# S4 convolution plus gated MLP on one core: early loads regrouped, GLU results accumulated into a copy of x, DMA transposes for half of the tokens, one more level of squares

## The chip, the cores and the metric

The kernel runs on one core of a Trainium2 chip. The core has five instruction streams: TensorE (PE, matrix products; its weight loads are listed apart as PEld), VectorE (DVE), ScalarE (ACT), GpSimd (POOL) and SyncE (SP, which here only issues DMAs). DMAs are issued from the queues of SP, ACT and POOL. The metric is the device time of one execution in microseconds (us), lower is better. The profile is of one execution, taken with the hardware profiler.

## The reference

The input `u` is a sequence of 2048 tokens with 512 channels in bfloat16. Cut to what matters:

```python
x = A_u                                   # (1, 2048, 512)
xn = _layernorm(x)
# branch A: a diagonal state space model with 128 modes per channel, as a long convolution
dt = exp(log_dt); P = exp(dt * (A_re + 1j*A_im) * l)      # l = 0..2047
K = einsum("dn,dnl,dn->dl", C, P, dt * B).real            # one kernel of 2048 taps per channel
yA = irfft(rfft(pad(xn)) * rfft(pad(K)))[:2048] + xn * Dskip
# branch B: a gated linear unit, 512 -> 1792 -> 512
yB = (sigmoid(xn @ w_gate) * (xn @ w_up)) @ w_down
return x + yA + yB
```

## The kernel before, in words

The program is a list of 1,266 tasks. Each is made with `_Plan.add`: an engine, a planned cost, a function that emits the instructions, and for some an alternative on another engine (`alt`). At the end they are emitted in the order that the tuple `TURN` lists, by task number; the tuple `OTHER` lists the tasks that take their alternative. Costs, ranks and `after` lists are for planning alone. Each engine executes its instructions in the emitted order, and the waits between engines come from the data: an instruction waits for what it reads, and for the buffer that it writes to be free. Buffers rotate: `zs` and `gs` share four buffers in SBUF, matmul results share four PSUM banks (`mbank`, pool `ps_m`), and the gate and up products have two pairs of banks of their own (`ps_gu`). A DMA from the SP or ACT queue takes one of eight semaphores in turn and waits until the DMA that had it eight issues before has landed; POOL's DMAs have eight of their own.

The stages, with the names and lines that matter below:

- **Loads** (`loads`, from line 356). `x` comes as `xg`, four groups of four token tiles of 128 rows. The S4 parameters come as `rawn` (A_re, A_im, B_re, B_im, C_re, C_im in slots 0 to 5), then the constants `ident`, `s1`, `s1e`, `s2`, `s2h`, `dsk`, and the GLU weights `W` (gate and up) and `wd` (down). POOL issues C, B, the constants and `dsk`.
- **Layer norm** (`layernorm`, from line 427). `stat` takes `bn_stats` of a tile on DVE (line 436). `rstd0` (lines 443 to 456) works out mean and inverse deviation for group 0 in small operations on DVE; `rstd` (lines 465 to 496) does the same for group 1 on POOL and for groups 2 and 3 together on DVE. `norm` (DVE, line 500) or `norm2` (ACT, line 505) normalises a tile in place. `turn` (line 510) transposes two tiles on PE into a PSUM bank `pt`, and an eviction writes them to `xnT`, the transposed input of the GLU, of which two buffers exist.
- **Parameters** (`params`). PE multiplies A and B by dt (`ptd`, `pb`) and transposes C (`ptp`); ACT and DVE make `exp` and `sin`/`cos` (`turns`, `frac`, `sincos`) of them, then the base rows of the tables in `B` and the multipliers in `M`.
- **Tables** (`tables`). For each of eight chunks of 64 channels the powers are built by doubling: `H` with 32 steps and `G` with 64 steps. A level is three DVE operations (`_level`, lines 1212 to 1214); `grow` replaces the even steps of the levels in `SQUARED` by squares, one ACT operation (line 859) and two on DVE (lines 861, 863). PE multiplies `G` by `H` into `pk` (line 947), which gives the convolution kernel, and on to its spectrum.
- **Spectrum of xn** (`spectrum_x1`, `spectrum_x2`). 32 products with `s1` give `pz`, evicted to `zs` and stored to `z_scr` in DRAM (SP); read back as `B<-z_scr` and multiplied again.
- **GLU** (`glu`, from line 741). Four groups, one after the other on PE: seven pairs of gate (`pg`) and up (`pu`) products of 128x512, sigmoid on ACT (line 778), product on DVE into `hT` (line 785), then `down` (line 756): for each tile 14 products of 128x512 into `po`, and one more with the identity that adds x itself, loaded again as `xt`. Of the 512 channels of `po`, the first 384 (`KEEP`) go through `gs` to the output (line 811, SP) and the last 128 stay on chip in `gl`.
- **Product and inverse** (`freq`, `outq`). The spectra are multiplied on DVE (line 1113), transformed back on PE (`pv`), and for the first 384 channels go through `v_scr` in DRAM and a product with `s2` (`py`, line 1172) to `M`, and from there by an accumulating DMA of POOL into the output (line 1192). The last 128 channels stay on chip: `vT` is transposed on PE into `ptv` (line 1157), copied, multiplied with `s2h` (line 1177), added to `gl` on DVE (line 1186), and `gl` is stored.

`evict` (lines 349 and 350) is the helper of nearly all copies out of PSUM: line 349 on ACT, line 350 on DVE. `dma` (line 342) is the helper of most DMAs.

## Time and profile before

| what | value |
|---|---|
| median of 3 runs | 268.0 us (266.95 to 268.19) |
| the profiled execution's own time | 269.39 us |
| its span, first to last event | 267.6 us |
| mean granted TensorE clock | 0.987 |
| DMA bytes | 43.05 MB, mean 161 GB/s |
| `out_dram<-gs`, SP | 32 issues of 48 KB, median 2.7 us to landing |
| `xt` loads, SP | 16 issues of 128 KB, median 3.3 us to landing |
| `out_dram<-M`, POOL | 24 issues of 64 KB, median 4.3 us to landing |

How to read it: a line of a group or a timeline gives the start and duration, or the busy time and mean of one, then the engine, the source line, the operation, and output<-input with shapes. "L350" is line 350 of the kernel before. The view by stage gives for each stretch the time in which each engine was busy, with the number of instructions in brackets. The chain of waits follows the work that ended last back to what released it.

### The profile page before, as it was taken

How to read it: one execution, taken by the hardware profiler on the slowest of the kernel's cores; microseconds unless marked ns; L12 is line 12 of the kernel's file. 1: busy time of each engine (PE TensorE's matmuls, PEld its weight loads, DVE VectorE, ACT ScalarE, POOL GpSimd, SP SyncE). 2: the span in 40 equal slices, each digit the busy share in tenths (PEclk: the TensorE clock that was granted, in tenths of full speed). 3: DMA queues.
4: the chain of work that ended last, by engine and by line, in shares of the span. 5: the costliest groups of instructions: out<-in, count | busy, mean ns of one | idle time of the engine just before them, and what ended most of it. 6: DMA issues, size and time to landing. Idle time of an engine off the chain costs nothing.

```text
span 267.6 us, 5570 instructions
## 1 busy us (share of the span) xinstructions
PE 236.7 (88%) x2039; PEld 136.9 (51%) x2064; DVE 246.8 (92%) x447; ACT 228.4 (85%) x362; POOL 48.1 (18%) x76
## 2 busy tenths in 40 slices
PE   0448999999999999899999999799999999969881
PEld 0325444444445544645545655565666576548660
DVE  2799999998999999999999999999999999998772
ACT  2669999999999886599999789899999889895860
POOL 9105982000000000000000000000000004436682
PEclk9999999999999999999999999999999999997997
DMA  6959981013801512225434489697989897997798
GB/s 162 249 142 315 316 253 50 0 40 88 345 20 40 179 48 63 76 94 150 148 98 118 110 227 229 160 270 188 252 215 281 201 219 167 223 242 138 98 133 88
DMA packets 68859, 43.05 MB, mean 161 GB/s; under 512 B 34704, under 2 KB 64416, under 8 KB 68320
## 3 DMA queue, kind: packets, MB, share of 16 engines
q1 hardware_dynamic: 63488, 39.99, 55.5%
q0 software_dynamic: 4896, 2.31, 8.0%
q10 hardware_dynamic: 448, 0.39, 0.7%
q8 instruction: 16, 0.26, 0.5%
q14 instruction: 11, 0.09, 0.1%
HBM read 24.33 MB, written 14.16 MB: 144 GB/s over the span
## 4 chain that ended last, share of the span: by engine, by line
PE 38%; DVE 25%; ACT 18%; DMA 10%; issue 5%; SPq 2%; ACTq 1%; DVEq 0%
PE pg L752 8%; PE pu L752 8%; PE po L756 7%; PE pk L947 4%; DMA B<-v_scr 4%; DMA zk_scr<-Z 3%; DVE tB L1212 2%; DVE stats L436 2%; DVE G L1213 2%; ACT M L349 2%; PE pv L1104 2%; ACT hT L778 2%; DMA rawn<-in_A_A_im_dram 2%; DVE G L1214 2%; DVE hT L785 2%
## 5 line engine op out<-in xcount | busy, mean ns | idle before, releaser
L752 PEld LDWEIGHTS <-W 128*128 128x128 bf16 x448 | 43.1, 98 | 50.9 <-issue 4.8
L1192 POOL DMA_DIRECT2D out_dram<-M x24 | 24.2, 1530 | 196.9 <-ACT M L349 191.2
L752 PE MATMUL pg<-xnT,W 128*128 128x512 bf16 x217 | 52.9, 384 | 1.0 <-ACT hT L778 0.3
L752 PE MATMUL pu<-xnT,W 128*128 128x512 bf16 x213 | 52.0, 379 | 0.9 <-DMA z_scr<-zs 0.2
L756 PE MATMUL po<-wd,hT 128*128 128x512 bf16 x217 | 51.6, 379 | 0.5
L756 PEld LDWEIGHTS <-hT 128*128 128x128 bf16 x224 | 21.6, 98 | 23.9 <-issue 0.4
L778 ACT ACTIVATE hT<-pg 128x1024 bf16<-128x1024 f32 x28 | 30.1, 1074 | 2.6 <-PE pg L752 1.2
L349 ACT ACTIVATE hT<-pu 128x1024 bf16<-128x1024 f32 x24 | 26.2, 1091 | 0.9 <-PE pu L752 0.8
L859 ACT ACTIVATE tB<-G 128x1024 bf16<-128x1024 bf16 (+1 forms) x17 | 24.5, 1442 | 2.7 <-DVE G L1214 1.5
L1214 DVE TENSOR_TENSOR G<-G,tB 128x1024 bf16<-128x1024 bf16 (+2 forms) x35 | 24.4, 702 | 0.4
L1213 DVE TENSOR_TENSOR G<-G,M 128x1024 bf16<-128x1024 bf16 (+1 forms) x42 | 22.0, 559 | 0.1
L947 PEld LDWEIGHTS <-G 128*128 128x128 bf16 x512 | 18.7, 100 | 5.9 <-DVE G L1214 2.7
L947 PE MATMUL pk<-H,G 128*128 128x64 bf16 x512 | 19.9, 196 | 1.9 <-DVE G L1214 0.9
L349 ACT ACTIVATE zs<-pz 128x512 bf16<-128x512 f32 x30 | 19.2, 670 | 2.4 <-PE pz L735 2.4
L1212 DVE TENSOR_TENSOR tB<-G,M 128x1024 bf16<-128x1024 bf16 (+2 forms) x27 | 21.0, 784 | 0.1
L1113 DVE TENSOR_TENSOR M<-XX,M 128x1024 bf16<-128x1024 bf16 x28 | 18.9, 686 | 0.3 <-ACT M L349 0.3
L1214 DVE TENSOR_TENSOR H<-H,tB 128x512 bf16<-128x512 bf16 (+2 forms) x24 | 18.6, 776 | 0.3
L349 ACT ACTIVATE M<-pkf 128x512 bf16<-128x512 f32 x28 | 17.9, 664 | 0.9 <-PE pkf L1093 0.9
L349 ACT ACTIVATE ksb<-pk 128x512 bf16<-128x512 f32 x28 | 17.3, 646 | 1.1 <-PE py L1172 0.5
L349 ACT ACTIVATE XX<-px 128x512 bf16<-128x512 f32 x26 | 16.0, 659 | 0.6 <-PE px L1046 0.5
L785 DVE TENSOR_TENSOR hT<-hT 128x1024 bf16<-128x1024 bf16 x24 | 16.3, 684 | 0.1
L1212 DVE TENSOR_TENSOR tB<-H,M 128x1024 bf16<-128x1024 bf16 (+1 forms) x16 | 15.2, 952 | 0.2
(211 smaller groups left out, 440.3 us busy)
## 6 DMA issues: line engine op xcount, KB each, us to landing
z_scr<-zs SPq DMA_DIRECT2D x32, 128.0 KB, 1.8
XX<-XX SPq DMA_DIRECT2D x28, 128.0 KB, 3.3
zk_scr<-Z SPq DMA_DIRECT2D x3, 1024.0 KB, 6.6
B<-zk_scr SPq DMA_DIRECT2D x12, 256.0 KB, 3.8
B<-v_scr SPq DMA_DIRECT2D x12, 256.0 KB, 4.0
xt<-in_A_u_dram SPq DMA_DIRECT2D x16, 128.0 KB, 3.3
B<-z_scr SPq DMA_DIRECT2D x8, 256.0 KB, 3.4
wd<-in_B_w_down_dram SPq DMA_DIRECT2D x1, 1792.0 KB, 14.4
```

The costliest lines, as they stand in the source:

```text
L349: return self.p.add("ACT", cost, lambda: nc.scalar.activation(out=dst(), in_=src(), func=ACT.Identity), alt=alt and ("DVE", alt[0], lambda ...
L752: nc.tensor.matmul(p[:, kk, :], w(kt, kk), xnT[:, kt, :], start=(kt == 0), stop=(kt == KT - 1))
L756: nc.tensor.matmul(po[:], hT[:, k, jj * 128:(jj + 1) * 128], wd[:, k, :], start=(k == 0), stop=False)
L778: e1 = add("ACT", 1.03, lambda hT=hT, k=k, pg=pg: nc.scalar.activation(out=hT[:, k:k + 2, :], in_=pg[:], func=ACT.Sigmoid), [m1] + held.ge ...
L785: prods.append(add("DVE", 0.69, lambda hT=hT, u=u, k=k: nc.vector.tensor_tensor(out=hT[:, k:k + 2, :], in0=hT[:, u:u + 2, :], in1=hT[:, k: ...
L859: a = add("ACT", 0.22 + 4 * h * k / 1200.0, lambda: nc.scalar.activation(out=sv(), in_=G[:, :, rs, src, :], func=ACT.Square, scale=float(2 ...
L947: nc.tensor.matmul(pk[:, r], G[:, comp, 8 * q + r].rearrange("p a h -> p (a h)"), H[:, comp, 8 * q + r].rearrange("p b h -> p (b h)"), sta ...
L1113: d = add("DVE", 0.69, lambda pp=pp, XX=XX, k1=k1, bs=bs: nc.vector.tensor_tensor(out=pp[:], in0=XX[:, :, bs, dx], in1=k1[:].to_broadcast( ...
L1192: self.p.add("POOL", 1.2, lambda j=j, o=o, ot=ot: nc.gpsimd.dma_start(out=o(), in_=ot[64 * j:64 * j + 64, :, :], accum_op=ALU.add), move=0 ...
L1212: lambda: [tt(out=tv()[:, c], in0=l[:, c], in1=mul[1][:, c], op=ALU.mult) for c in cs],
L1213: lambda: [tt(out=inner(o[:, c]), in0=inner(l[:, c]), in1=both(c), op=ALU.mult) for c in ones],
L1214: lambda: [tt(out=o[:, c], in0=o[:, c], in1=tv()[:, flip(c)], op=ALU.add) for c in cs],
```

## The change

- `loads`: POOL gets two tiny copies into a new tile `held`, which read the first group of x and the slots of A_re and A_im. In the new order they stand ahead of POOL's loads of C, B, `s1`, `s1e`, `s2` and `dsk`, which so are issued when x and A have landed.
- `layernorm`: tiles 1 and 3 may take their statistics on ACT (`stat_act`: a pass with a sum, a tiny scaling, a pass of squares with a sum), and do. The deviations of groups 2 and 3 move from DVE to POOL. The transposes of groups 2 and 3 are 32 transposing DMAs of 128x128 on SP, from `xg` straight to `xnT`; groups 0 and 1 keep PE and the eviction.
- `glu`: one DMA copies the first 384 channels of x from the input to the output in DRAM (`copied`, SP). The residual product with the identity covers the last 128 channels alone, and `xt` is loaded with these alone, once a group. `gs` is added to the output by accumulating DMAs of POOL, 32 of them, in place of SP's stores.
- `tables`: `SQUARED` gains the level 8, so one more ACT square per chunk and operations of half the size on DVE.
- `outq`: for the last two blocks `ptv` uses the GLU's banks and the copy out of it three buffers of its own (`vn`); `gl` is stored once for both blocks, in four DMAs of 128 channels, two of them on ACT.
- `TURN` and `OTHER` are new. `OTHER` now gives DVE eight of the `gl` evictions (one before), two `gs`, five `G<-B` copies (two before) and more of the parameter copies; PSUM evictions of 512 go from 29 to 31 on DVE.

```diff
-SQUARED = (16, 32)
+SQUARED = (8, 16, 32)
...
+        held = c.tile([128, 8], BF, name="held")
...
+        def hold():
+            self.nc.gpsimd.tensor_copy(out=held[:, 0:4], in_=self.xg[0][:, 0:4, 0])
+            self.nc.gpsimd.tensor_copy(out=held[:, 4:6], in_=self.rawn[:, 0:2, 0])
...
         for q in (4, 5, 2, 3):
-            raw(q, "POOL", after=["raw0", "raw1"])
+            raw(q, "POOL", after=["hold"])
...
+        def stat_act(i):
+            xi, f = self.xg[0][:, i, :], ACT.Identity
+            nc.scalar.activation(out=self.junk[:], in_=xi, func=f, scale=1.0 / D, accum_out=mv[:, i, 0:1])
+            nc.scalar.activation(out=off[:, i:i + 1], in_=mv[:, i, 0:1], func=f, scale=-float(D) ** -0.5)
+            nc.scalar.activation(out=self.junk[:], in_=xi, func=ACT.Square, scale=float(D) ** -0.5, bias=off[:, i:i + 1],
+                                 accum_out=mv[:, i, 1:2])
...
+            slow = lambda lo=lo, hi=hi: rstd(lo, hi, nc.gpsimd)
+            r = add("POOL", 20.0, slow, st, R["LN2"] + 10 * lo) if lo == 1 else add(
                 "DVE", 4.2 if lo else 3.4, (lambda lo=lo, hi=hi: rstd(lo, hi, nc.vector)) if lo else rstd0, st, R["LN2"] + 10 * lo if lo else R["LN"],
+                alt=("POOL", 16.0, slow, R["LN2"] + 10 * lo) if lo else None)
...
+                if g > 1:
+                    self.norm += n
+                    for k in range(2):
+                        for kt in range(KT):
+                            new = i % 4 == 0 and k == 0 and kt == 0
+                            self.xT.append(self.p.add("SP", 1.25, lambda i=i, k=k, kt=kt, g=g: nc.sync.dma_start_transpose(
+                                out=xnT[g][:, kt, (i % 4 + k) * 128:(i % 4 + k + 1) * 128], in_=self.xg[g][:, i % 4 + k, kt * 128:(kt + 1) * 128]),
+                                n, rank, take=[xnT[g]] if new else [], use=[self.xg[g]] + ([] if new else [xnT[g]]), move=0.3))
+                    continue
...
+        copied = self.p.add("SP", 0.55, lambda: self.nc.sync.dma_start(out=self.out[0][:, 0:KEEP], in_=self.u[0][:, 0:KEEP]), [ldwd],
+                            rank=96, move=6.0)
...
-                nc.tensor.matmul(po[:], self.ident[:], xt[:, jj % 2, :], start=False, stop=True)
+                nc.tensor.matmul(po[:, KEEP:], self.ident[:], xt[:, jj, :], start=False, stop=True)
...
-                self.gw[i] = [self.p.add("SP", 1.1, lambda i=i, gs=gs: [nc.sync.dma_start(
-                    out=self.ov[j][:, i, 0:KEEP], in_=gs[64 * j:64 * j + 64, 0:KEEP]) for j in range(2)], move=0.33, after=[e],
-                    rank=base + 9, use=[gs])]
+                self.gw[i] = [self.p.add("POOL", 2.4, lambda i=i, gs=gs: [nc.gpsimd.dma_start(
+                    out=self.ov[j][:, i, 0:KEEP], in_=gs[64 * j:64 * j + 64, 0:KEEP], accum_op=ALU.add) for j in range(2)], move=0.6,
+                    after=[e, copied], rank=base + 9, use=[gs])]
...
-            vp = self.mview("vp", 2, "p (g d) -> p g d", d=nd if wide else 128)
+            vp = self.mview("vp", 2, "p (g d) -> p g d", d=nd) if wide else self.mview("vn", 3, "p (g d) -> p g d", d=128)
...
-                    pt = self.mbank([128, 4, 128], F32, "ptv")
+                    pt = self.buf("ps_gu", [128, 4, 128], F32, "ptv", 2, "gu")
...
+                self.ended.setdefault((g, j), []).extend(es)
+                if k == len(BLOCKS) - 1:
+                    self.dma("SP", lambda j=j, g=g: self.ov[j][:, ni * g:ni * g + ni, KEEP:],
+                             lambda j=j, g=g: self.gl[64 * j:64 * j + 64, ni * g:ni * g + ni, :], 0.065, 0.11, after=self.ended[g, j],
+                             rank=rk, either=True)
...
-    4, 5, 85, 84, 1, 0, 3, 6, 7, 2, 86, 14, 27, 15, 34, 87, 88, 33, 90, 9, 89, 32, 98, 8, 96, 100, 11, 12, 95, 22,
+    4, 5, 110, 109, 1, 6, 7, 0, 3, 2, 111, 15, 28, 16, 21, 34, 112, 35, 113, 37, 36, 114, 121, 13, 115, 8, 38, 119,
...
```

## The prediction

> **What bounds it now.** I read, in this order, the page, busy time by stage, then the start, GpSimd and the end as timelines. Of the page: engine shares and the chain of work that ended last.
>
> ```profile
> PE 236.7 (88%) x2039; PEld 136.9 (51%) x2064; DVE 246.8 (92%) x447; ACT 228.4 (85%) x362; POOL 48.1 (18%) x76
> PE 38%; DVE 25%; ACT 18%; DMA 10%; issue 5%; SPq 2%; ACTq 1%; DVEq 0%
> ```
>
> The busiest engine is DVE, but the shares are means over unlike stages. Busy time by stage (start:end, length, then PE, PEld, DVE, ACT, POOL with instruction counts, TensorE clock, DMA share, GB/s):
>
> ```profile
> 0.00:13.00 13.00, 2.92 (x16) 2.18 (x16) 5.94 (x19) 5.80 (x11) 6.91 (x17) 1.00 0.85 202
> 13.00:23.00 10.00, 5.62 (x29) 3.91 (x30) 9.38 (x28) 7.35 (x11) 0.66 (x4) 1.00 0.72 183
> ...
> 241.26:267.60 26.34, 18.16 (x352) 14.12 (x349) 17.34 (x32) 13.51 (x25) 15.32 (x16) 0.89 0.86 112
> 22.94:241.26 218.32, 210.10 (x1647) 116.71 (x1672) 214.20 (x372) 201.78 (x318) 25.22 (x43) 1.00 0.61 163
> ```
>
> Three stages: a start of 23 us in which nobody is full; a middle of 218.3 us, from the first `db` product to the last table level, where DVE is idle 4.1 us and PE 8.2; and 26.3 us after it, a chain of short steps at a clock of 0.89. In the middle DVE is the bound, so work given to DVE costs its length, and work taken off PE or ACT pays only where DVE had waited.
>
> The start, on DVE:
>
> ```profile
> 10.30 0.69 DVE L436 BATCH_NORM_STATS2 stats<-xg 128x6 f32<-128x512 bf16 x1
> 11.12 0.66 DVE L436 BATCH_NORM_STATS2 stats<-xg 128x6 f32<-128x512 bf16 x1
> 12.03 0.17 DVE L443 CAST m_b<-mv 128x4 bf16<-128x4 f32 x1
> 15.31 1.06 DVE L500 TENSOR_SCALAR xg<-xg,m_f,rinv 128x512 bf16<-128x512 bf16 x3
> 22.17 0.67 DVE L350 COPY xnT<-pt 128x1024 bf16<-128x1024 bf16 x1
> ```
>
> Tiles 2 and 3 get statistics only at 10.30 and 11.12, so group 0's deviations run 12.03 to 15.31 and its `xnT` is whole at 22.84; the first gate product starts at 23.06.
>
> GpSimd, computing group 1's deviations on four columns:
>
> ```profile
> 26.20 0.20 POOL L484 TENSOR_TENSOR rinv<-q,rinv 128x4 f32<-128x4 f32 x1
> 26.48 0.58 POOL L477 TENSOR_TENSOR q<-rinv 128x4 f32<-128x4 f32 x1
> 27.13 2.13 POOL L482 TENSOR_TENSOR q<-q,ve_f 128x4 f32<-128x4 f32 x1
> 29.35 2.11 POOL L483 TENSOR_SCALAR q<-q 128x4 f32<-128x4 f32 x1
> ```
>
> A 0.2 us operation takes 2.1 us while DVE runs its float32 products of 2.3 us. The end, on SP:
>
> ```profile
> 239.58 1.24 SPq L811 DMA_DIRECT2D out_dram<-gs  x2
> 244.91 9.51 SPq L342 DMA_DIRECT2D B<-v_scr  x4
> 254.64 10.03 SPq L342 DMA_DIRECT2D out_dram<-gl  x8
> ```
>
> **The sum** is made against the profiled execution's own 269.39 us (span 267.6), 0.5% above the median 268.0; at the end I take off 1.4.
>
> *Start.* Statistics of tiles 1 and 3 go to ACT: two passes and a small one, 0.66 + 0.2 + 0.66 each (rows of the 512-wide eviction and of the tiny activation; ACT's idle stretch of 3.68 us before 8.60 covers the first). DVE loses two statistics and aggregations, 2 x (0.68 + 0.18) = 1.7 us, and the `turns` pair, which waits for `A_im` (now ACT's fourth load instead of its third, +0.5 on 7.53), no longer stands ahead of tile 2. I place the deviations at 8.7 to 12.0, 3.3 earlier. Behind them stand norms, transposes, `frac` and `xnT`; on the work in between the gain shrinks: first gate product near 21.5, -1.6 us. Against that, `C`, `B`, `s1`, `s1e` and `s2` sit behind a wait on GpSimd until x's first group and `A_re`, `A_im` have landed, about 7.5 (`A_im` landed at 7.53). The four raw loads took 6.7 to 8.1 us to land beside x and W; with those ahead landed I take 5. Then `s1`, `C` and `B` are there by about 13, 15 and 17; PE used `C` at 11.63, `s1` at 15.77 and `B` at 20.93. Ends: -1.6, or 0 if they land in 8 us (rival two).
>
> *DVE in the middle.* Removed: the 24 operations of groups 2 and 3's deviations, 42.88 to 47.13, -4.25. Third square level: per chunk three 1024-wide operations at 0.645 (two back to back take 1.29) become two 512-wide at 0.38 and four 256-wide at about 0.25, 1.94 to 1.76, times 8 is -1.4. Two norms more, 2 x 0.41 = +0.8. Evictions and copies changed from ACT to DVE: `gl` +7 x 0.29, `gs` +2 x about 0.5 (between 0.29 and 0.69), `G<-B` +3 x 0.29, 512-wide evictions from PSUM +10 -8 at 0.69, parameter copies net about +1.0: together +6.3. With the statistics the total is -0.2. But 1.4 of savings lies ahead of the first `db` product, and the new order has about 1.2 us less DVE work after the last table level, so work that filled idle time at both ends now lies in the full stretch: +2.4 us there.
>
> *What DVE's idle 4.1 us may give back.* PE loses 32 transposes (four blocks at 0.45) and 16 residual products shrink from 512 to 128 columns (0.216 to 0.055): -1.8 - 2.6 = -4.4. ACT loses four `xnT` evictions (-4.1), two norms (-1.65) and the evictions named (about -9), gains the squares (8 x 0.65 = +5.2) and statistics (+3.0): about -6.8. Neither is the bound; they can only end DVE's waits, between 0 and -4.1. I take -2, the middle, since ACT at 92% and PE at 96% are near enough to full to cause most of those waits.
>
> *GpSimd.* Groups 2 and 3's deviations, 33 operations on eight columns, start after group 1's, about 42.5. Uncontended, one each 0.28 us: done at 51.7. Blocked once by a 0.69 DVE operation each: 33 x 0.97 = 32, done at 74.5. In group 1 four of 33 were blocked for over 2 us and the whole took 18.0; at that pace it is done at 60.5, which I take. The first norm that waits for it is ACT's 71st instruction; by the counts in the stages ACT had done 50 at 45 us and 80 at 65, so it gets there at about 59: 0 us, ends 0 and +4 (rival one). The 32 GLU stores come to GpSimd as accumulating DMAs: 32 x 1.03 (the row of `out<-M` in runs) = 33 us on an engine idle from 41 to 224. They land in about 4.3 instead of 2.7 us, which holds a `gs`/`zs` buffer 1.6 us longer, of four: 0.
>
> *SP.* Off: 32 stores at 0.6 and eight `xt` loads at 0.55, -23.6 us. On: 32 transposing DMAs, which no row shows: between 0.36 (cheapest issue) and 1.8 each (the landing of `z_scr`, if nothing overlaps), 12 to 58 us. SP's other issues between 60 and 141 come to some 18 us, so 81 us hold 2.0 each: 0. The copy of x into the output, 1.5 MB, lands by 8 to 14 us (1 MB: 6.6; `wd` 1.75 MB: 14.4), before the first `gs` at 58.7 and beside a DMA share of 0.11 from 45 to 65: 0.
>
> The Trainium skill ("Advanced Engine Details and Errata", X-Bar Transpose) says that on trn2 a transposing DMA is as fast as a regular one; no run here shows it yet. By that each would cost like a plain issue, 32 x 0.55 = 17.6, and the sum stays as it is.
>
> *End.* Eight `out<-gl` in series, the last landing 3.0 after 264.7, become two on SP and two on ACT: after the last `gl` addition (262.65) 0.6 + 0.6 + 3.0 gives 266.9, and GpSimd's last store (262.59 + 4.3) ends there too: -0.7. Before that the `ptv` banks come from the free GLU pair and `vn` has three buffers: 0 to -1, taken -0.3.
>
> Sum: -1.6 + 2.4 - 2.0 - 0.7 - 0.3 = -2.2, so 267.2 for such an execution and **265.8** against the median.
>
> **Rivals.** *One, it is slower: GpSimd's deviations come late.* ACT waits in order on them, and behind it stand the hT evictions of PE's next group. It decides from about 60 on. Done at 67, halfway to the worst, ACT stands 7 us; PE's two pairs of banks, 1.9 us each, cover some 3, the other 4 reach PE and DVE, and the 2 us of idle regained are lost with them: 265.8 + 6 = 271.8. For it: four rows over 2 us in group 1. Against it: from 45 to 65 DVE works in pieces of 0.4 to 1.2, not 2.3. The Trainium skill ("SBUF — State Buffer", Who interferes with whom) has a DVE operation with two SBUF inputs contend with any GpSimd operation that reads SBUF; by that nearly every one of the 33 would be held, the late end above. The rows agree only in part: most of group 1's took 0.2 us beside a DVE that was never idle.
>
> *Two, the held loads eat the start.* Landing in 8 us, `B_re` arrives near 20 and `C` at 18 and the first gate product stays at 23: 265.8 + 1.6 = 267.4. For it: landings of 6.7 to 8.1; against: `s1e`, issued alone, landed in 2.1.
>
> *Three, DVE is the bound outright:* none of the 4.1 us comes back, 267.8.
>
> *Four, the transposes are slow.* Above 2.0 us each on SP, `z_scr` is late, then `B<-z_scr` (141.1), then the first spectrum products; each 0.1 us more is 3.2 us, with PE's third `down` from 142.8 as 20 us of cover at best. At 2.7 each it is 22 us late, 2 uncovered, and group 3's `xnT` is pressed as well: about +4, 270.
>
> *Five, more than forecast:* all idle regained and a shorter end, -2.1 - 1: 262.7.
>
> **Chances.** Forecast 0.40 (own range 264 to 267.3), five 0.10, three 0.17, two 0.10, one 0.13, four 0.10. Half a per cent, 1.3 us, is about what a measurement tells from no change: under 266.7 is faster, over 269.3 slower. Faster: 0.36 + 0.10 = 0.46; same: 0.04 + 0.12 + 0.07 = 0.23; slower: rest of three and two 0.08 + 0.23 = 0.31. The range 262 to 271.5 cuts the worse half of one and tails of four and five.
>
> **What would show it.** Deviations of group 0 ending near 12, first gate product near 21.5; raw `B` landed before PE asks; GpSimd's second deviations done by 60 and no ACT wait on POOL; transposes under 2 us on SP; last table level near 240 with DVE idle below 3 us from the first `db`; the last landing under 5 us after the last addition. Wrong if ACT waits for POOL, if the first `z_scr` read slips past 145, or if the accumulating stores hold `gs` evictions.

## The result, and the profile after

The changed kernel takes 275.35 us (median; 274.71 to 276.35) against 267.89 us (266.95 to 268.19) for the kernel before on the same chip: a ratio of 1.0288, 95% interval 1.0244 to 1.0332. It is slower by 2.9%, 7.5 us, and lies outside the predicted range of 262 to 271.5. Its profiled execution has 274.85 us of its own and a span of 273.1. One execution reported below, 278.34 us of the kernel with `gs` back on SP in the new order, was in the slower of two states that the chip shows, and is left out of its median and ratio.

From its page, the engine shares and the chain of work that ended last:

```profile
PE 235.8 (86%) x2032; PEld 136.2 (50%) x2032; DVE 246.8 (90%) x462; ACT 224.2 (82%) x357; POOL 87.8 (32%) x143
DVE 9%; PE 6%; ACT 3%; DMA 1%; POOL 1%; issue 1%; POOLq 0%; DVEq 0%; ACTq 0%
```

DVE's total is the same 246.8 us as before; only the span around it has grown. The shares hide the loss, so the stages come next, by the same bounds as in the prediction (start:end, length, then PE, PEld, DVE, ACT, POOL with instruction counts, TensorE clock, DMA share, GB/s):

```profile
0.00:13.00 13.00, 2.07 (x8) 1.12 (x8) 5.73 (x26) 8.72 (x19) 6.05 (x17) 1.00 0.89 201
13.00:21.64 8.64, 6.28 (x38) 4.86 (x39) 8.31 (x17) 5.63 (x9) 2.68 (x9) 1.00 0.65 171
21.64:242.80 221.16, 207.54 (x1630) 114.87 (x1629) 216.45 (x392) 194.83 (x304) 61.60 (x104) 0.99 0.67 165
242.80:273.10 30.30, 19.94 (x363) 15.34 (x360) 16.26 (x29) 15.04 (x28) 17.47 (x18) 0.84 0.77 116
```

Set against the kernel before (22.94, then 218.32, then 26.34):

| stage | before | after | difference | forecast |
|---|---|---|---|---|
| start, to the first `db` product | 22.94 | 21.64 | -1.3 | -1.6 |
| middle: DVE's work | 214.20 | 216.45 | +2.25 | +2.4 |
| middle: DVE's idle time | 4.1 | 4.7 | +0.6 | -2.0 |
| after the last table level | 26.34 | 30.30 | +4.0 | -1.0 |

That is +5.5, the difference of the two profiled executions (274.85 - 269.39). The other 2.0 up to 7.5 is where they lie to their medians: the one of before 1.5 above, the one of after 0.5 below.

The start in the timeline (start, duration, engine, line, operation; in brackets the idle time before it and who ended it):

```profile
6.89 0.19 POOL L402 COPY held<-xg 128x4 bf16<-128x4 bf16 x1 [4.11 <-DMA xg<-in_A_u_dram]
9.01 0.18 POOL L403 COPY held<-rawn 128x2 bf16<-128x2 bf16 x1 [1.93 <-DMA rawn<-in_A_A_im_dram]
...
12.62 0.78 DVE L516 TENSOR_SCALAR xg<-xg,m_f,rinv 128x512 bf16<-128x512 bf16 x2
...
15.36 1.46 PE L764 MATMUL pz<-xg,s 128*128 128x512 bf16 x3 [5.39 <-DMA s<-c_s]
```

GpSimd is held until 9.2; the first normalisation starts at 12.62 instead of 15.31; but PE, which could go on then, stands until `s1` is there at 15.36. The first gate product starts at 21.81, and no row has PE waiting for raw `B`.

GpSimd's second set of deviations, and the ACT instruction that needs it:

```profile
42.98 0.32 POOL L481 TENSOR_TENSOR agg<-stats 128x16 f32<-128x16 f32 x1 [6.38 <-DVE stats L445]
...
58.97 0.47 POOL L512 TENSOR_TENSOR nb<-agg,rinv 128x8 f32<-128x8 f32 x1
...
59.47 2.93 ACT L521 ACTIVATE xg<-xg,nb,rinv 128x512 bf16<-128x512 bf16 x4
```

Done at 59.44, used at 59.47. ACT's instruction ahead of it had ended at 59.36, so ACT stood about 0.1 us for the deviations: they are only just in time. The end, on PE, POOL and SP:

```profile
257.44 4.13 POOL L1223 DMA_DIRECT2D out_dram<-M  x4 [3.24 <-DVE M L351]
...
260.98 0.41 PE L1203 MATMUL py<-B,s 128*64 128x512 bf16 x2
...
262.40 4.12 POOL L1223 DMA_DIRECT2D out_dram<-M  x4 [0.83 <-ACT M L350]
...
263.13 0.41 PE L1203 MATMUL py<-B,s 128*64 128x512 bf16 x2
...
263.25 1.77 SPq L343 DMA_DIRECT2D out_dram<-gl  x2
```

GpSimd stands for 3.24 us, then issues the last eight `out<-M` by 266.52, while the last `gl` addition is over at 264.35. In the kernel before GpSimd's last issue ended with the last addition (262.59 and 262.66). POOL's queue ends the program with an instruction called `DRAIN` (count, then min/median/max in ns):

```profile
L1356 POOLq DRAIN  x3: 46/108/7402, 264.9 to 272.8; - x3
```

The longest lasts 7.40 us, where the kernel before had 5.78. It ends at 272.28, 3.1 us behind the last packet that any queue moved (269.17, a store of `M`), so these 3.1 us move no data. In the kernel before the drain ended 1.83 us behind its own queue's last packet, and together with the last packet of the other queues (266.13 and 266.04).

### The profile page after: what moved, and what is told of

The parts are those of the page before. It is cut to its first block, busy times and chain, and to the rows that moved or that the text cites. A ratio compares the mean times of both kernels' runs of the same rounds, so it can differ in the third digit from the quotient of the medians.

```text
span 273.1 us, 5591 instructions
## 1 busy us (share of the span) xinstructions
PE 235.8 (86%) x2032; PEld 136.2 (50%) x2032; DVE 246.8 (90%) x462; ACT 224.2 (82%) x357; POOL 87.8 (32%) x143
## 5 line engine op out<-in xcount | busy, mean ns | idle before, releaser
L842 POOL DMA_DIRECT2D out_dram<-gs x32 | 29.1, 1268 | 121.1 <-ACT gs L350 48.7
L1223 POOL DMA_DIRECT2D out_dram<-M x24 | 26.5, 1715 | 33.9 <-ACT M L350 30.7
L787 PEld LDWEIGHTS <-hT 128*128 128x128 bf16 x224 | 21.7, 99 | 23.8 <-issue 1.1
L890 ACT ACTIVATE tB<-G 128x1024 bf16<-128x1024 bf16 (+2 forms) x25 | 29.4, 1177 | 3.0 <-DVE G L892 2.3
L1248 DVE TENSOR_TENSOR G<-G,tB 128x512 bf16<-128x512 bf16 (+2 forms) x35 | 22.3, 642 | 0.5
L1247 DVE TENSOR_TENSOR G<-G,M 128x512 bf16<-128x512 bf16 (+2 forms) x50 | 20.4, 450 | 0.2
L350 ACT ACTIVATE zs<-pz 128x512 bf16<-128x512 f32 x29 | 17.0, 606 | 3.0 <-PE pz L764 3.0
L1246 DVE TENSOR_TENSOR tB<-G,M 128x512 bf16<-128x512 bf16 (+2 forms) x27 | 18.8, 703 | 0.2
L350 ACT ACTIVATE ksb<-pk 128x512 bf16<-128x512 f32 x27 | 15.8, 604 | 3.5 <-PE pk L980 3.3
L1132 PE MATMUL pv<-M,w 128*128 128x256 bf16 (+1 forms) x128 | 14.0, 250 | 3.6 <-DVE M L1144 3.5
L764 PE MATMUL pz<-xg,s 128*128 128x512 bf16 x32 | 11.9, 410 | 5.4 <-DMA s<-c_s 5.4
```

The source lines that it names most:

```text
L350: return self.p.add("ACT", cost, lambda: nc.scalar.activation(out=dst(), in_=src(), func=ACT.Identity), alt=alt and ("DVE", alt[0], lambda ...
L787: nc.tensor.matmul(po[:], hT[:, k, jj * 128:(jj + 1) * 128], wd[:, k, :], start=(k == 0), stop=False)
L842: self.gw[i] = [self.p.add("POOL", 2.4, lambda i=i, gs=gs: [nc.gpsimd.dma_start(out=self.ov[j][:, i, 0:KEEP], in_=gs[64 * j:64 * j + 64, 0 ...
L890: a = add("ACT", 0.22 + 4 * h * k / 1200.0, lambda: nc.scalar.activation(out=sv(), in_=G[:, :, rs, src, :], func=ACT.Square, scale=float(2 ...
L1223: self.p.add("POOL", 1.2, lambda j=j, o=o, ot=ot: nc.gpsimd.dma_start(out=o(), in_=ot[64 * j:64 * j + 64, :, :], accum_op=ALU.add), move=0 ...
L1246: lambda: [tt(out=tv()[:, c], in0=l[:, c], in1=mul[1][:, c], op=ALU.mult) for c in cs],
```

## The experiments

The theory after the result: the end is lost by the order of the last wide `py` products, which puts GpSimd's last stores late; the middle is lost by DVE's longer work. Rivals: the accumulating DMAs on GpSimd, the transposing DMAs on SP, and GpSimd's deviations, each forecast at 0 us. In the diffs below, task numbers in `TURN` are shown with what they are.

### The end

The eight tasks of the last two wide products (product, eviction, two stores each) go ahead of the last block's first `ptv`:

```
 TURN
+    1224, 1225, 1227, 1226, 1219, 1220, 1221, 1222   (py, evict, out<-M of block 1: g=3 j=1, g=2 j=1)
     1284                                             (first ptv of block 3)
-    ... the same eight, among the last 30 tasks
```

> The changed kernel with the last two wide py products, their evictions and their four stores (k=1, g=2 and g=3) moved ahead of the first transposes of vT, where PE was idle 0.4 us and ACT 1.2. Theory 'their late place in the order sets the end': both evictions are done by 261 instead of 262.1 and 264.2, GpSimd's last issue ends near 265 instead of 266.5, and the whole is 1 to 2 us faster. Rival 'GpSimd's queue is full there anyway (eight issues of 1.03 us from 257.4)': the last issue ends at 265.7 at best and the gain is under 0.8 us; a third, 'the last gl additions become the end': no gain, they slip by 0.8.

Measured: 276.35 us, ratio 1.0302 (1.0234 to 1.0369). No gain, and the end stage is 30.86 us long. The last `M` issues did not come earlier, 23.7 us from the last table level as before the edit: GpSimd still stood 3.24 us ahead of 259.21, waiting for an `M` eviction on DVE, and then had eight stores to issue at 1.03 us each. Two products alone move the wait, not the queue. So all of block 1's late wide products go earlier, with their reads of `v_scr`, and two evictions from DVE to ACT:

```
 TURN
+    1209, 1210, 1223, 1214, 1215, 1218               (py g=0 and g=1 j=1 of block 1, reads of v_scr)
     1264                                             (a product of freq, block 3)
+    1211, 1212, 1216, 1217                           (their out<-M)
     1279                                             (a later product of freq, block 3)
+    1224, 1225, 1227, 1226, 1219, 1220, 1221, 1222   (as above)
     1248                                             (first ptv of block 2)
 OTHER
-    1210, 1215                                       (evictions of py: DVE to ACT)
```

> The changed kernel with all four last wide py products (the second block) moved forward by about 5 us, as soon as their loads have landed, two of their evictions on ACT in place of DVE, and their eight stores on GpSimd behind them, so that GpSimd isn't idle from 254.2 to 257.4. Theory 'the end is GpSimd's queue of eight stores that starts too late': GpSimd's last issue ends 2 to 4 us sooner counted from the last table level (23.7 us now), the end comes when the gl stores land, and the whole is 1.5 to 3 us faster. Rival 'PE's last chain sets the end': the two products pushed into PE's chain move the last gl additions by 0.9 us or more and the whole gains nothing.

Measured: 271.77 us, ratio 1.0169 (1.0115 to 1.0223). By the ratios this is 1.2% less than the changed kernel (1.0288 - 1.0169, with the two intervals put together +-0.7%), 3.6 us by the medians. Its stages and GpSimd's end (two views, stages first):

```profile
22.15:243.36 221.21, 206.26 (x1630) 114.31 (x1628) 216.45 (x393) 195.39 (x305) 61.43 (x104) 0.99 0.67 166
243.36:270.20 26.84, 19.64 (x363) 14.79 (x360) 15.52 (x27) 15.90 (x30) 17.54 (x18) 0.88 0.87 131
```

```profile
250.54 8.12 POOL L1223 DMA_DIRECT2D out_dram<-M  x8 [1.88 <-ACT M L350]
259.16 4.12 POOL L1223 DMA_DIRECT2D out_dram<-M  x4 [0.50 <-ACT M L350]
```

GpSimd's 3.24 us of standing is gone, eight stores follow each other from 250.5, and the last issue ends 19.9 us after the last table level instead of 23.7. The stage is 26.84 long instead of 30.30, nearly the 26.34 of the kernel before; the middle is what it was (221.21 to 221.16). So most of the loss at the end comes from the place of these tasks in the order: moving them, with the two evictions, gave 3.5 of its 4.0 us back. The drain did not get shorter (8.34 us), but it now ends with the landing of the last `gl` stores (268.83 and 268.67), so it adds hardly anything. What is left, 3.9 us against the kernel before, is for the larger part not at the end.

### GpSimd's accumulating stores and the copy of x

Put alone into the kernel before:

```
-                lambda i=i, gs=gs: [nc.sync.dma_start(out=..., in_=gs[...])
+                lambda i=i, gs=gs: [nc.gpsimd.dma_start(out=..., in_=gs[...], accum_op=ALU.add)
+            nc.sync.dma_start(out=self.out[0][:, 0:KEEP], in_=self.u[0][:, 0:KEEP])     (right behind the load of wd)
-                nc.tensor.matmul(po[:], self.ident[:], xt[:, jj % 2, :], ...)
+                nc.tensor.matmul(po[:, KEEP:], self.ident[:], xt[:, jj % 2, KEEP:], ...)
```

> The kernel before with one part of the change: x copied into the output behind the load of wd, the residual product cut to the last 128 channels, the GLU results accumulated by GpSimd in place of SP's stores; the order of all work is that of before. Theory 'the accumulates cost the end': PE's 2.6 us less bring nothing in the middle, where DVE is full; GpSimd's drain grows from 5.8 to 7 us or more and its stores of M stand behind late gs stores, the whole 1 to 2.5 us slower than before. Rival 'only the new order costs the end': within 0.7 us of before, or faster by PE's 2.6 us.

Measured: 271.35 us, ratio 1.0139 (1.0087 to 1.0192), 3.5 us slower. Its stages, and the drain of POOL's queue:

```profile
21.55:240.57 219.02, 209.06 (x1673) 115.93 (x1673) 214.44 (x373) 201.44 (x319) 50.37 (x74) 1.00 0.66 171
240.57:268.20 27.63, 18.11 (x349) 13.88 (x346) 17.34 (x32) 13.53 (x25) 17.28 (x18) 0.87 0.83 108
```

```profile
L1321 POOLq DRAIN  x3: 46/103/7793, 259.6 to 267.9; - x3
```

Against the kernel before the middle is 0.7 longer and the end 1.3; the drain is 7.79 instead of 5.78 although GpSimd's last issue ends with the last `gl` addition, as before. Here the drain ends 4.0 us behind its queue's last packet (1.83 before) and 2.1 behind that of the others. This profiled execution is the quickest of its kernel, so the 2 us that it shows are not all of the 3.5.

In the changed kernel, the other way round: `gs` goes back to plain stores on SP, and the copy is dropped.

```
-                self.p.add("POOL", 2.4, lambda i=i, gs=gs: [nc.gpsimd.dma_start(..., accum_op=ALU.add)
+                self.p.add("SP", 1.1, lambda i=i, gs=gs: [nc.sync.dma_start(...)
-        copied = self.p.add("SP", 0.55, lambda: self.nc.sync.dma_start(out=self.out[0][:, 0:KEEP], ...), [ldwd],
+        copied = self.p.add("SP", 0.55, lambda: None, [ldwd],
```

> The changed kernel with the GLU results stored by plain DMAs of SP as before, and no copy of x into the output; this leaves x out of the first 384 channels of the output. GpSimd then issues 24 stores instead of 56. Theory 'GpSimd's queue sets the end': GpSimd's drain after its last issue falls from 7.4 to about 5.8 us and the stores of M before the end are issued sooner, so the tail shrinks from 30.3 to 27.5 to 29 us and the whole is 1.5 to 3 us faster. Rival 'the end is set by the order of the last py products, whoever stores': drain and tail as they are, the whole within 0.7 us of the changed kernel.

Measured: 274.35 us, ratio 1.024 (1.0159 to 1.0321): no gain that can be told. The drain is 6.35 us, ends 1.83 us behind its queue's last packet instead of 3.12, and the stage after the last table level is 28.87 long, 1.4 less. So in this order `gs` on GpSimd's queue does cost at the end. But the middle is 223.71, 2.6 more. Of these, 1.6 are a wait of DVE for `hT` behind a stretch from 30.0 to 33.4 in which TensorE was granted half its clock (the last section has more on this). The same edit on the kernel with the earlier products:

> The changed kernel with the last wide py products early (as in the sixth run) and the GLU results stored by plain DMAs of SP without the copy of x; this leaves x out of the first 384 channels of the output. Theory 'the end has two parts, the order of the last products and the accumulates': the drain falls by 1 to 2 us, the tail from 26.8 to 25.5 to 26, and the whole is 1 to 2.5 us faster than the sixth run's 271.8. Rival 'with the products early the accumulates are hidden': within 0.7 us of it.

Measured: 275.75 us, ratio 1.025 (1.0197 to 1.0304), so 0.8% worse by the ratios than with the accumulating stores (4.0 us by the medians, which were not taken on the same chip). From the waits (total us, times, longest):

```profile
ACT zs L350 <- DMA z_scr<-zs: 2.8, 1, 2.8
DVE hT L816 <- ACT hT L350: 3.5, 1, 3.5
```

SP, now with 32 stores and 32 transposes, is late with a store of `zs`; ACT stands for the buffer, and DVE behind ACT. (TensorE's granted clock was also 0.50 from 122.0 to 125.4, beside that wait; the run does not part the two.) That mixes two things, the kind of the store and its queue. The last pair keeps the queue. With the earlier products, `gs` stays on GpSimd, but is stored plainly:

```
-                    ..., in_=gs[64 * j:64 * j + 64, 0:KEEP], accum_op=ALU.add) for j in range(2)], move=0.6,
+                    ..., in_=gs[64 * j:64 * j + 64, 0:KEEP]) for j in range(2)], move=0.6,
-        copied = ... lambda: self.nc.sync.dma_start(out=self.out[0][:, 0:KEEP], in_=self.u[0][:, 0:KEEP]), [ldwd],
+        copied = ... lambda: None, [ldwd],
```

> The same kernel with gs stored by GpSimd as plain DMAs, same number, same queue, same places, and no copy of x into the output before them, so that x is left out of the first 384 channels. Only the accumulation and the copy go; GpSimd's and SP's other work stays. If the accumulation itself (reads beside the writes, longer landings, a longer drain of GpSimd's queue at the end) is what cost 3.4 us when it was put into the kernel before, 268.5 to 270 is expected and a final drain of under 7 us. If it is the place on GpSimd's queue, or nothing, 271 to 272.5 and the same drain.

Measured: 271.6 us, ratio 1.0134 (1.0058 to 1.0209), beside 271.77 with the accumulation. The drain is 8.34 us in both. So in this order neither the accumulation nor the copy has a price that can be told from none, and the longer drain does not come from accumulating. It goes rather with how many DMAs are on GpSimd's queue: with `gs` on SP and then on GpSimd it was 5.78 and 7.79 us in the order of before, 6.35 and 7.40 in the changed kernel, and 7.37 and 8.34 with the earlier products.

### The transposing DMAs

With the earlier products, each transposing DMA is replaced by a plain one of the same block:

```
-    lambda i=i, k=k, kt=kt, g=g: nc.sync.dma_start_transpose(
+    lambda i=i, k=k, kt=kt, g=g: nc.sync.dma_start(
```

> The kernel of the run in which all of the last wide products were earlier (271.8 us), with its 32 transposing DMAs of groups 2 and 3 replaced by plain DMAs of the same 128x128 blocks from the same tile to the same tile, in the same places (groups 2 and 3 of the GLU get untransposed tokens, so the transposition is left out). If what is left of the loss (3.9 us against the kernel before) comes from the transposes holding SP (1.1 to 1.3 us each where a plain issue takes about 0.55, so some 20 us of SP), 268 to 270 is expected, with the stores of zs earlier. If the transposes are hidden, as the forecast had it at 0 us, 271 to 272.5.

Measured: 272.05 us, ratio 1.0137 (1.0077 to 1.0197), beside 271.77: nothing gained. What SP spends on them, in the changed kernel and then in this one (ns, min/median/max):

```profile
L549 SPq DMA_TRANSPOSE xnT<-xg x32: 1093/1224/2557, 60.3 to 146.8; - x32
DMA to landing us min/median/max: 2.2/2.6/6.3
```

```profile
L549 SPq DMA_DIRECT2D xnT<-xg x32: 465/592/2362, 60.2 to 146.7; - x32
DMA to landing us min/median/max: 1.7/2.5/6.5
```

A transpose holds SP for 1.22 us instead of 0.59 and lands as quickly, so it is 20 us more of SP in all; spread over the order as they are, they are hidden. With both edits at once:

> Both of these edits together (transposition left out for groups 2 and 3, x left out of the first 384 channels). If each has its own share, the gains add; if SP and the accumulation press the same transfers, the sum is less than the two. If neither matters, 271 to 272.5 again, and what is left of the loss lies in the work of DVE in the middle stage, forecast at 2.4 us, and in the order of the work itself.

Measured: 271.48 us, ratio 1.0108 (1.0051 to 1.0165). Taken away together, accumulation and transposition leave the loss within 0.3 us of where it was by the medians; by the ratios 0.6% is gained (+-0.8%). So neither of these two rivals has a loss here that can be told from none, though a small share is not excluded. Its stages:

```profile
21.46:241.63 220.17, 205.98 (x1628) 114.25 (x1628) 216.49 (x393) 194.88 (x304) 52.50 (x106) 0.99 0.59 158
241.63:268.20 26.57, 19.62 (x363) 14.60 (x360) 15.53 (x28) 15.93 (x30) 17.02 (x17) 0.89 0.84 131
```

The place matters, though. In the kernel before, with the deviations of groups 2 and 3 on GpSimd (next section), the transposes were put in four blocks of eight, where the evictions of `xnT` had been:

```
-                t = add("PE", 0.67, lambda i=i, pt=pt: turn(i, pt), ...)      (and its eviction)
+                if g > 1:      eight nc.sync.dma_start_transpose in one task, at the eviction's place
```

> The kernel of the run before this one with a second part of the change: the transposes of groups 2 and 3 as 32 DMAs on SP (8 in the place of each of four evictions), so PE loses 32 transposes (1.8 us) and ACT four evictions (4.1 us). Theory 'SP has the room, and PE's and ACT's time are worth little beside a full DVE': the DMAs take 1.1 to 1.3 us of SP each, no gate product waits for them, and the whole is within 1 us of the run before this one. Rival 'each block of eight holds SP for 10 us and z_scr's stores behind it, which hold zs buffers': 1 to 4 us slower, with ACT or PE waiting on zs.

Measured: 292.69 us, ratio 1.0868 (1.0823 to 1.0913), 23 us slower. From SP's timeline, and from the waits:

```profile
167.50 10.18 SPq L529 DMA_TRANSPOSE xnT<-xg  x8
177.80 0.58 SPq L342 DMA_DIRECT2D zk_scr<-Z  x1
178.48 4.00 SPq L342 DMA_DIRECT2D M<-z_scr  x1
```

```profile
DVE M L1124 <- DMA B<-zk_scr: 10.2, 1, 10.2
PE pg L763 <- DMA xnT<-xg: 8.9, 8, 2.3
```

Eight in a row hold SP for 10 us. The store of `zk_scr` is queued behind them, DVE waits 10.2 us for the reads that follow it, and PE waits for each landing of `xnT`. That is rival four's mechanism. It was to decide from 2.0 us each, by the room that SP has in all; eight in a row decide at 1.3 (10.18 / 8), because the room is counted between two issues that others wait for.

### The deviations on GpSimd, and the hold

The two tiny copies that hold GpSimd's loads are left out:

```
         def hold():
-            self.nc.gpsimd.tensor_copy(out=held[:, 0:4], in_=self.xg[0][:, 0:4, 0])
-            self.nc.gpsimd.tensor_copy(out=held[:, 4:6], in_=self.rawn[:, 0:2, 0])
+            pass
```

> The changed kernel without the two small copies on GpSimd, so its loads of C, B and the constants are issued at once. Theory 'the hold costs at the start': s1 is there before the first norm ends, the first pz product starts near 13.1 instead of 15.36, the first gate product at 20 to 20.8 instead of 21.81, and the whole is 1 to 1.5 us faster. Rival 'the hold pays': x's first group lands later, deviations of group 0 end after 12.5 and the first gate product comes at 22 or later; the whole is the same or up to 1 us slower.

Measured: 279.85 us, ratio 1.0427 (1.0352 to 1.0501), 4.5 us slower than the changed kernel. The first `pz` came at 13.76 instead of 15.36, since `s1` was there; but the first gate product came later, at 22.58 instead of 21.81. The larger part lies elsewhere, in two rows of GpSimd's timeline and two of the waits:

```profile
43.51 3.57 POOL L481 TENSOR_TENSOR agg<-stats 128x8 f32<-128x8 f32 x1
...
48.01 2.45 POOL L483 TENSOR_TENSOR agg<-agg 128x8 f32<-128x8 f32 x1
```

```profile
ACT xg L520 <- POOL nb L511: 5.7, 1, 5.7
PE pg L782 <- ACT xnT L350: 4.0, 1, 4.0
```

Two operations, of 0.39 and 0.31 us in the changed kernel, took 6.0 together, the deviations were done at 64.04 instead of 59.44, and ACT and then PE stood for them. This is rival one, in a kernel beside the changed one. The middle was 226.40 long, 5.2 more.

The same deviations back on DVE, in the changed kernel:

```
 OTHER
-    68        (deviations of groups 2 and 3: GpSimd to DVE)
```

> The changed kernel with the deviations of groups 2 and 3 back on DVE, 24 small operations, 4.25 us there before; nothing else moves. Theory 'DVE is full in the middle, so its work counts in full': the last table level comes 3 to 4.3 us later than 242.8 and the whole is 3 to 4 us slower than the changed kernel (278 to 279.5). Rival 'the middle isn't DVE's alone, and GpSimd's deviations come so near the norm that waits for them that some executions lose by it': 0 to 2 us slower, or faster, with the spread of its executions smaller than the 1.6 us of the changed kernel.

Measured: 279.67 us, ratio 1.046 (1.0412 to 1.0508): 4.3 us more, for the 4.25 us that these operations took on DVE in the kernel before.

```profile
21.58:248.29 226.71, 209.21 (x1638) 114.81 (x1637) 219.85 (x418) 195.98 (x305) 47.53 (x73) 0.98 0.65 162
```

DVE's work in the middle is 3.4 more and the stage 5.5. Of the difference, 1.4 are a wait of DVE for `hT` behind a half-clock stretch of TensorE, from 29.0 to 32.4. The mirror image, from DVE to GpSimd in the kernel before:

```
-    ... (lambda lo=lo, hi=hi: rstd(lo, hi, nc.vector)) if lo else rstd0 ...
+    ... (lambda lo=lo, hi=hi: rstd(lo, hi, nc.gpsimd)) if lo else rstd0 ...
 TURN
+    69        (normalisation of tile 9 ahead of that of tile 8)
     68
```

> The kernel before with one part of the change: groups 2 and 3's deviations on GpSimd in place of DVE's 24 operations (4.25 us), and the first norm that needs them moved from 60.6 us back to the next one, at 69.2. Theory 'work on DVE counts in full, both ways, as long as nobody waits for GpSimd': GpSimd runs from about 43 to 58 or 62, no norm waits for it, the last table level comes 3 to 4 us sooner and the whole is 2.5 to 4 us faster than before (264 to 265.5). Rival 'DVE's time comes back only where ACT and PE have room': 0 to 1 us faster, DVE's idle time in the middle grows by about 3.

Measured: 269.33 us against 268.98, ratio 0.9995 (0.9963 to 1.0027): nothing. Stage and waits:

```profile
22.23:240.57 218.34, 210.07 (x1641) 116.76 (x1666) 210.79 (x347) 201.50 (x318) 36.26 (x76) 1.00 0.60 163
```

```profile
DVE hT L785 <- ACT hT L349: 3.8, 2, 2.4
```

DVE has 3.4 us less to do (210.79 to 214.20), and the middle is as long as it was (218.34 to 218.32). The time turned into waits for ACT, which the kernel before has no row of. They end at 44.66 and 48.89, about where the deviations had stood on DVE (42.88 to 47.13). So in these runs work put on DVE lengthened the middle, but work taken off it did not shorten it.

### DVE's other work

The evictions and copies that the new `OTHER` had moved from ACT to DVE go back:

```
 OTHER
-    315, 320, 325, 422, 427, 432, 483, 493    (gl evictions)
-    372, 377                                  (gs evictions)
-    654, 703, 856                             (G<-B copies)
```

> The changed kernel with 13 copies taken back from DVE to ACT in the same order of work: all eight gl evictions, both gs evictions and three G<-B copies. DVE loses 8 x 0.29 + 2 x 0.5 + 3 x 0.29 = 4.2 us, ACT gains 8 x 0.28 + 2 x 0.49 + 3 x 0.68 = 5.3 us. Theory 'DVE is the bound of the middle': the last table level comes about 3 to 4 us sooner than 242.8 and the whole is 2 to 4 us faster than the changed kernel (about 272). Rival 'ACT is as full where these copies stand': no gain or slower (275 to 278), with longer waits of PE for ACT. The tail (30.3 us from the last table level) stays in both.

Measured: 275.78 us, ratio 1.0277 (1.0202 to 1.0352): no change.

```profile
21.47:241.70 220.23, 205.93 (x1605) 114.92 (x1628) 214.24 (x380) 197.86 (x318) 61.28 (x105) 0.99 0.66 166
```

DVE's work is back at the 214.2 of the kernel before, but the stage is 220.23, not 218.3: idle time took the place of more than half of it (6.0 instead of 4.7). The third level of squares is dropped, and the level built in whole on DVE:

```
-SQUARED = (8, 16, 32)
+SQUARED = (16, 32)
```

> The changed kernel without the third level of squares: the level of eight is built whole on DVE as before (per chunk three 1024-wide operations for two of 512 and four of 256), no square on ACT for it; the order of the rest stays. DVE gains 8 x 0.18 = 1.4 us, ACT loses 5.2. Theory 'DVE is full': the whole is 1 to 2 us slower than the changed kernel. Rival 'the chain over ACT within a level costs DVE waits': the same or faster, with fewer waits of DVE and ACT in the tables.

Measured: 278.8 us against 268.98, ratio 1.0355 (1.0314 to 1.0396), by the ratios 0.7% above the changed kernel (+-0.6%).

```profile
21.66:246.07 224.41, 206.38 (x1605) 114.89 (x1629) 219.23 (x368) 191.65 (x296) 61.98 (x105) 0.99 0.66 163
```

2.8 us more on DVE, 3.2 us more of the middle: by this trace the third squares pay.

### The start

In the kernel before, the statistics of tiles 2 and 3 go ahead of the `turns` pair that waits for `A_im`:

```
 TURN
+    35, 36    (statistics of tiles 2 and 3)
     100       (turns)
```

> The kernel before with the statistics of tiles 2 and 3 moved ahead of the turns pair on DVE, which waits 1.5 us for ACT; nothing else moves. Theory 'the start's gain is worth its length': the deviations end 1.2 to 1.5 us sooner, the first db product comes at 21.5 to 21.9 instead of 22.94, and the whole is 1 to 1.5 us faster than before. Rival 'a DVE that comes earlier to the first db product waits there or in the next stage for ACT, whose sines end when they ended': no change.

Measured: 268.04 us, ratio 1.002 (0.9994 to 1.0045): no change, though its first `db` product is at 21.44. The reason is in executions that did not touch the start at all. In the kernel before and in the three made from it above, DVE has the same first instructions; here is the product that waits for `A_im`, and the first `db` product, in the kernel before and in the one with the accumulating stores:

```profile
9.23 0.43 DVE L605 TENSOR_SCALAR sq<-sq 128x512 f32<-128x512 f32 x1 [1.46 <-ACT sq L597]
...
22.94 0.69 DVE L627 TENSOR_TENSOR db<-raw,pb 128x512 f32<-128x512 bf16 x1
```

```profile
8.02 0.43 DVE L605 TENSOR_SCALAR sq<-sq 128x512 f32<-128x512 f32 x1 [0.92 <-ACT sq L597]
...
21.55 0.68 DVE L627 TENSOR_TENSOR db<-raw,pb 128x512 f32<-128x512 bf16 x1
```

(With the deviations on GpSimd these were 8.52 and 22.23, with the transposes there as well 9.05 and 22.77.) So the start of the kernel before wanders by 1.4 us with the landing of its loads, and its profiled execution had the latest of the four.

## Why the prediction was wrong

Most of its single prices held; the two gains that were to pay for DVE's longer work did not come, and one of them had the wrong sign.

- **Start, -1.6.** Its mechanism held: the deviations ended at 12.5 (forecast 12.0), the first gate product started at 21.81 (21.5), and the held loads caused no wait at the gate, so rival two did not come. One part was off: `s1`, forecast for about 13, was there at 15.36, because the hold lasted until 9.2 instead of 7.5, and PE stood 5.4 us for it. The size was taken against a late execution. The four executions with the old start have the first `db` product at 21.55 to 22.94, 22.4 in the mean; the eleven of the new order that keep the changed start and the hold have it at 21.46 to 22.15, 21.7 in the mean. So the usual gain is about 0.7 us. The last step of the sum then took 1.4 us off, because that execution lay above the median. As its start was 0.6 later than the mean of the four, a part of the same time was counted as a gain twice.
- **DVE in the middle, +2.4.** Right in the sum, +2.25, but not in its terms, whose errors cancel. Leaving the third squares out cost 2.8 of DVE's time (forecast 1.4). Taking the 13 moved evictions and copies back took 2.2 off DVE in the middle, where 4.2 had been priced. The deviations were 3.4 there (forecast 4.25). What made up the rest is not worked out.
- **Idle given back, -2.0.** This failed: +0.6. The step reasoned that PE and ACT, relieved by 4.4 and 6.8 us, would end DVE's waits. PE and ACT were relieved (207.54 and 194.83 of work, from 210.10 and 201.78), and DVE's waits stayed. That is rival three by its number, and 2.6 us of the miss; its reason, that DVE alone sets the length of the middle, does not hold, since taking 3.4 us off DVE in the old order gave nothing, and taking 2.2 off in the new one gave 0.9. In the new order the middle is 220.2 to 222.8 us long (all kernels that put no work on DVE or SP and do not wait for GpSimd's deviations), whether DVE has 214.2 or 216.5 us to do in it; in the old order it is 218.1 to 219.0, with 210.8 or 214.4. What sets these two lengths besides DVE's work is not settled: no single wait accounts for it. That TensorE was granted half its clock for longer in the new order (last section) is a rival that no run here tests.
- **GpSimd's deviations, 0.** Right in size, and by luck as to the margin: done at 59.44, ACT's instruction started at 59.47. In all ten traces of the new order with these deviations on GpSimd and the hold, ACT's first normalisation starts 0.03 to 0.04 us behind GpSimd's last operation. The run without the hold shows the other side of the edge. The forecast's bounds of 51.7 and 74.5 were wide enough, and its 60.5, taken by group 1's pace, was close.
- **GLU accumulates and the copy, 0; transposes, 0.** Right, as far as can be told, in the order with the earlier products: without both, 0.3 us less. In the changed kernel itself the drain was 1.05 us longer with `gs` on GpSimd's queue, and the end stage 1.4; the sum had no term for a drain. The bound of 0.36 to 1.8 us for a transpose held the measured 1.22. The Trainium skill ("Advanced Engine Details and Errata", X-Bar Transpose) has it as fast as a regular DMA: for the landing the traces agree (2.6 to 2.5 us), for SP's time they don't (1.22 to 0.59).
- **End, -0.7 and -0.3.** This failed by most, and is the step that made the forecast wrong: +4.0. The step said that GpSimd's last store, at 262.59 in the kernel before, would end "there too". It priced the `gl` stores and the buffers, and took GpSimd's place from the old order. The new order puts the last wide products among and behind the last `ptv`, and GpSimd's last store with them: 23.7 us from the last table level instead of 21.3, and the drain behind it is 1.6 longer. Putting them earlier, with two evictions moved to ACT, gave 3.5 us of the stage back. No rival had this.

The forecast for the profiled execution was 267.2, and it took 274.85: 7.7 us more, of which 2.6 are the idle time and 5.0 the end. The other 1.9 up to the medians (265.8 and 275.35) is the last step, which took 1.4 off where 0.5 was to be added.

The kernel with the earlier products is still 3.9 us above the kernel before; by the profiles some 3 of them lie in the middle (221.2 to 218.3) and 0.5 at the end. Of the 3.5 us that the accumulating stores cost in the old order the profile shows 2.0. The rest is open in both; how much of the 3.9 is due to the granted clock no run tells.

None of the kernels beat the kernel before.

## What to carry to other kernels

When a change brings a new order with it, price the last instructions of every queue by their new places, above all those that start a DMA: here GpSimd's late last stores, with the drain behind them, cost 4.0 us where the whole change was to gain 2.2. An idle time next to a busy engine is not a reserve: in these runs adding work there lengthened the stage by at least as much (5.5 us for 3.4, of which 1.4 stood behind a half-clock stretch; 3.2 for 2.8), and removing 3.4 us gave nothing, because waits for ACT took its place. Before a difference of a few us is laid to the order, set the granted clocks of the two kernels side by side as well. And if the profiled execution lies above the median, find the stage in which it does before crediting a gain in that stage.

## What the runs showed that was not expected

- The drain of POOL's queue lasted 5.67 to 7.37 us at the end where it had stored `M` alone (24 DMAs), and 7.40 to 9.75 us with the 32 of `gs` as well, whether these accumulated or not (8.34 in both). It ended 1.8 to 2.1 us behind the queue's last packet with `M` alone, and 3.1 to 4.0 with `gs` as well. In the changed kernel this is the end of the whole; with the earlier products it is hidden. Why earlier DMAs should matter is not shown.
- The same two GpSimd operations on eight columns took 0.39 and 0.31 us in one kernel and 3.57 and 2.45 in another, the first of them 0.25 us apart in its start. The Trainium skill ("SBUF — State Buffer", Who interferes with whom) has DVE operations with two SBUF inputs contend with GpSimd operations that read SBUF. Beside the operation of 3.57 us DVE ran five two-input operations in a row (43.72 to 46.80); in the changed kernel the same five ran beside GpSimd operations of 0.5 to 0.7 us. So the same operation can take nine times as long in another kernel, and how long it takes can't be read off one trace for another.
- The clock granted to TensorE differs between the orders. In slices of 1 us, the kernel before has one stretch at 0.50 while PE works, 3.4 us long (from 240.2). The changed kernel has 10.2 us of it (212.5 to 215.9 and 239.8 to 246.6), and the other kernels of the new order 6.8 to 17.1. One such stretch has a price on record: in the kernel with the last `py` products earlier (the first run above) it lies at 29.8 to 33.2, eight gate products took 3.14 us there instead of 1.89, DVE then waited 1.6 us for `hT`, and the middle is 1.6 us longer than in the changed kernel, whose order is the same up to there. What the stretches near 212 and 240 cost, and why the new order has more of them, is not shown.
